# One unit's low parts by products, 2-unit turns, early loads of block 0, and array halves exchanged for odd head pairs

## The chip, the cores and the metric

The kernel runs on one core of a Trainium2 chip. The metric is the time of one execution on the device in microseconds (us). Engines are named as the profile names them: PE (TensorE, matmuls), PEld (its weight loads), DVE (VectorE), ACT (ScalarE), POOL (GpSimd) and SP (the queue that issues the DMAs).

## What is computed

A decayed linear attention and two feed-forward layers, one behind the other, in float32:

```python
def _attn_ref(q, k, v, alpha):                    # (4, 8, 768, 48) each
    for t in range(S):
        state = alpha[:, :, t, :, None] * state + einsum('bhd,bhe->bhde', k[:, :, t], v[:, :, t])
        y[:, :, t] = einsum('bhd,bhde->bhe', q[:, :, t], state)
x = y.transpose(0, 2, 1, 3).reshape(3072, 384)
x = (x @ w_a) * (x @ w_b) @ w_out                  # d_ff 1536
h = x @ w_in                                       # d_ff 2048
out = (maximum(h, 0) + alpha2 * minimum(h, 0)) @ w_out2
```

The weights come as float64.

## The kernel before

**Tiling.** The 3072 tokens are six blocks (`NB`) of 512. A block is four chunks (`BC`) of 128 time steps, one for each batch, and a chunk holds all 8 heads as 4 pairs (`NJ`). The index `g` counts the 24 chunks. In a chunk a head of a pair lies on partitions 0 to 47, the other on 64 to 111.

**Precision of the matmuls.** The feed-forward layers work on values that are split in a high and a low float32r part; `mm3` adds high*high, low*high and high*low, so a matmul of 128x128 by 128x512 is three instructions. The attention's products are plain float32: in the compiled program each is two passes, one right behind the other, so 8 products show as 16 records.

**First layer.** The weights of `w_a`, `w_b` and `w_out` are cut in 6 units (`NU1`), each of two column groups of 128. A step `k` is one column group for one block: `pa` and `pb` (9 matmuls each, `up`), their product, and 9 matmuls into three accumulators (`down1`), two steps later (`LAG`). `SEGMENTS` says in which turns the steps go: block 0 with units 0 to 2 (6 steps), block 1 with the same, both with units 3 to 5, then blocks 2 to 5 with all 6 units each. At the end of a turn `evict1` copies or adds the three accumulators to a partial sum (`part`), or splits them for the second layer.

**Weights of the first layer.** `conv` turns a float64 unit of a weight into the high and the low part: ACT takes a magnitude (L253), DVE makes four passes (`sign`, `main`, `power`, `rest`, L256 to L270), ACT rounds to the high part (L276). The low part comes in one of two ways. With `on_pe` false, DVE makes two more passes (`sub` L279, `low` L282). With `on_pe` true, PE makes a sum in PSUM (`add`, L307 to L309: identity times c1, minus identity times the high part, identity times c2) and ACT copies it (L312), in two halves for each weight. `on_pe` holds for the units 0, 1 and 2 (`PE_UNITS = 3`), each with its three weights a, b and o. Weights a and b of unit 0 are converted in two column halves; their raw words lie in the slots of weights that are needed last.

**Attention of a chunk.** DVE makes two scans and a product (`scan_r` L387, `recip`, `scan_a` L397, `mul` L402); PE transposes k (`pe_k` L440, evicted by ACT), makes A = k q (`pe_a` L457, two banks) which DVE masks (`ev_a` L464, twice), makes the change of the state (`pe_d` L481), and y (`pe_y`): `intra` (L491) is v times As with a contraction over 128, `inter` (L497) is the state Z times q with a contraction over 48. Head `i` of a pair reads partitions from 64*i and writes partitions from 64*i of one bank. ACT and DVE split y into the block's x (L564, L568). Block 0 has no `inter`; its fourth pair comes through `vg` (L508). Block 1 is `moved`: its fourth pair goes first and is brought to its place by a product with `shift` (L533). In blocks 1 to 5 kps, A0, A1, dS and y take turns on three banks (`ps_att`); in block 0 kps, A0 and A1 lie in the accumulators' banks.

**Order.** An own planner (`Graph.run`) orders all operations of all engines when the program is built: each has an estimated duration, its dependencies and a key; of those that are ready, the one with the lowest key goes first. The keys follow from `SEGMENTS`: step `k` has `at[k]`, a weight is due at the first step that uses it, and a chunk's key is `block_at[n] - (BC - c) * 7500 - 6000`. `fill` puts dummy matmuls (`wp`, L184) where the plan has PE idle. On the chip each engine goes through its list in that order.

Of the kernel before, what the change touches and what calls it, by code (L numbers as in the profile page):

```python
# [21 lines left out]
P = 128  # L22
# [5 lines left out]
    (0, 0, 3), (1, 0, 3), (0, 3, 6), (1, 3, 6),  # L28
# [4 lines left out]
PE_UNITS = 3  # L33
# [105 lines left out]
def body(tc, akq, v, vg, w_a, w_b, w_o1, w_in, w_o2, beta, out):  # L139
# [13 lines left out]
    with ExitStack() as ctx:  # L153
# [6 lines left out]
        ps_att = pool("ps_att", 3, space=PSUM)  # L160
# [62 lines left out]
        def conv(src, tag, name, key, wait, sink, early=15000, on_pe=False, halves=None):  # L223
# [14 lines left out]
            for n in range(2 if halves else 1):  # L238
# [61 lines left out]
                for h in range(2 // N):  # L300
                    cut = lambda x, h=h: x[:, :, h * UC // 2 : (h + 1) * UC // 2] if N == 1 else x
                    p = {}

                    def add(p=p, cut=cut, c1=c1, c2=c2, hi=hi):
                        t = ps_mm.tile([P, MB], F32, name="cl", tag="mm")
                        o = p["t"] = t[:, 0 : UC // 2].rearrange("p (t f) -> p t f", t=nt)
                        nc.tensor.matmul(o, ident, cut(c1()), start=True, stop=False)  # L307
                        nc.tensor.matmul(o, minus, cut(hi()), start=False, stop=False)
                        nc.tensor.matmul(o, ident, cut(c2()), start=False, stop=True)  # L309

                    def low_pe(p=p, cut=cut, lo=lo):
                        nc.scalar.copy(cut(lo()), p["t"])  # L312
                        sink(b["r"])

                    y = G.add("PE", 900, add, key, [x], pool=mpool)
# [9 lines left out]
        done, slot_of, taken = {}, {}, {}  # L325
        for u in range(NU1):
            for nm, src in (("a", w_a), ("b", w_b), ("o", w_o1)):
                x = nm, u
                slot_of[x] = len(slot_of)
                uses[x] = []  # L330

                def sink(r, x=x):
                    units[x] = as_unit(r, 2 if x[0] == "o" else KT)


                spare = {("a", 0): 3 * NU1 - 1, ("b", 0): 3 * NU1 - 2}.get(x)
                ld, done[x] = conv(src[u], f"w{slot_of[x]}", f"{nm}{u}", due[x] - 20000,
                                   taken.pop(slot_of[x], ()), sink, on_pe=u < PE_UNITS,
                                   halves=None if spare is None else (f"w{spare}", KT))
                if spare is not None:  # L340
                    taken[spare] = done[x]
# [5 lines left out]
        aring, kring, sring, yring = Ring(3), Ring(1), Ring(1), Ring(1)  # L347
# [4 lines left out]
        def chunk(g):  # L352
# [9 lines left out]

            def load_a():
                s["ra"] = tp.tile([P, 2 * NA - 1], F32, name="ra", tag="ra")
                nc.sync.dma_start(s["ra"][:, NA - 1 :], akq[g, :, 0:NA])

            def load_kq():
                s["kq"] = tp.tile([P, 2, NJ, CH], F32, name="kq", tag="kq")
                nc.sync.dma_start(s["kq"].rearrange("p s j t -> p (s j t)"), akq[g, :, NA:])
# [11 lines left out]
            la = A("SP", 800, load_a, rring.take(), 14000, 2500)  # L381
            lq = A("SP", 1500, load_kq, lring.take(), 13800, 2500, [la])
# [26 lines left out]
            rring.use(k1)  # L409
# [3 lines left out]
            if not start:  # L413
                def decayed():
                    z = Z[:, c, :, :]
                    nc.vector.tensor_tensor(out=z, in0=z, in1=r0().to_broadcast([P, NJ, D]),
                                            op=ALU.mult)

                zs = A("DVE", 360, decayed, [r, *state[c]])
                rring.use(zs)  # L420

            def ps_tile(nm, bank=None):
                if start and bank is not None:
                    return ps_acc.tile([P, NJ, CH], F32, name=nm, tag=f"acc{bank}")
                return ps_att.tile([P, NJ, CH], F32, name=nm, tag="att")

            def bank(i):

                if start:
                    w, accfree[i] = accfree[i], []  # L430
                    return w, accfree[i]
                w = aring.take()
                return w, aring.last()

            ks = None
            if not end:
                def pe_k():
                    s["kps"] = ps_tile("kps", 0)
# [7 lines left out]
                w, hold = bank(0)  # L446
# [3 lines left out]
                lring.use(x)  # L450

            def pe_a():
                s["A"] = [ps_tile(f"A{i}", i + 1) for i in range(2)]
                for j in range(NJ):
                    for i in range(2):
                        ps = slice(64 * i, 64 * i + D)
                        nc.tensor.matmul(s["A"][i][:, j, :], kT()[ps, j, :], qT()[ps, j, :],  # L457
                                         start=True, stop=True)

            def ev_a(i):  # L460
                def f():
                    s["As", i] = tp.tile([P, NJ, CH], F32, name=f"As{i}", tag=f"As{i}", bufs=1)
                    m = mask.rearrange("p (o t) -> p o t", o=1).to_broadcast([P, NJ, CH])
                    nc.vector.tensor_tensor(out=s["As", i], in0=s["A"][i], in1=m, op=ALU.mult)  # L464
                return f

            (w0, h0), (w1, h1) = bank(1), bank(2)
            pa = A("PE", 1300, pe_a, [k1, q1, *w0, *w1])
            w = sring.take()
            a0 = A("DVE", 660, ev_a(0), [pa, *w], 0, slack)  # L470
            a1 = A("DVE", 660, ev_a(1), [pa, *w], 0, slack)
            h0.append(a0)
            h1.append(a1)

            if ks is not None:
                def pe_d():
                    s["dS"] = ps_att.tile([P, NJ, D], F32, name="dS", tag="att")
# [6 lines left out]
                ds = A("PE", 500, pe_d, [ks, lv, *aring.take()])  # L484
                dhold = aring.last()
                kring.use(ds)
# [12 lines left out]

            def pe_y():  # L500
                s["y"] = ps_tile("y")
                if start:

                    for j in range(KT):
                        intra(j, j == 0, False)
                    for j in range(KT):
                        for i in range(2):
                            nc.tensor.matmul(s["y"][64 * i : 64 * i + 64, j, :], s["vg"][:, j, i, :],  # L508
                                             s["As", i][:, KT, :], start=False, stop=j == KT - 1)
# [5 lines left out]
                for j in range(NJ):  # L515
                    intra(j, j == 0, False)
                for j in range(NJ):
                    inter(j, j == NJ - 1)

            py = A("PE", 1350 if start else 500 if moved else 1600, pe_y, [a0, a1, lv, q1, zs, *aring.take()])  # L520
            yhold = aring.last()
            if moved:
                def ev_3():
                    s["y3"] = shift[:, KT, :]
                    nc.scalar.copy(s["y3"], s["y"][:, KT, :])

                def pe_m():
                    for j in range(KT):
                        intra(j, j == 0, False)
                    for j in range(KT):  # L530
                        inter(j, False)
                    for j in range(KT):
                        nc.tensor.matmul(s["y"][:, j, :], shift[:, j, :], s["y3"], start=False,  # L533
                                         stop=j == KT - 1)

                x = A("ACT", 280, ev_3, [py, *yring.take()])
                py = A("PE", 1900, pe_m, [x])
                yring.use(py)
            lring.use(pa, py)
# [20 lines left out]

            def split_h():
                if c == 0:
                    xt[n] = xpool.tile([P, 2, NJ, MB], F32R, name="x", tag="x")
                nc.scalar.copy(xt[n][:, 0, 0:nt, cols], s["y"][:, 0:nt, :])  # L564

            def split_l():
                h, l = (xt[n][:, i, 0:nt, cols] for i in range(2))
                nc.vector.tensor_tensor(out=l, in0=s["y"][:, 0:nt, :], in1=h.bitcast(F32),  # L568
                                        op=ALU.subtract)
# [146 lines left out]
        for k, (n, i, s) in enumerate(flat):  # L716
# [4 lines left out]
                            [d for j in range(k - 1) for d in done["o", flat[j][1] // 2]  # L721
                             if flat[j][1] // 2 < PE_UNITS and k < 12] + [up_before])
# [135 lines left out]
def layout(q, k, v, alpha, moe_w_a, moe_w_b, moe_w_out, moe2_w_in, moe2_w_out, moe2_alpha):  # L858
# [6 lines left out]
    def padded(x, fill):  # L865
# [12 lines left out]
    vg = np.zeros((B, CH, H * D // P, 2, 64), v.dtype)  # L878
    vg[..., D:] = (
        v[:, H - 2 :, :CH].reshape(B, 2, CH, H * D // P, 64 - D).transpose(0, 2, 3, 1, 4)  # L880
    )

    KT, GR = H * D // P, 64 - D
    rows = np.concatenate([
        np.concatenate([np.arange(D) + (2 * t + i) * D, np.arange(GR) + (2 * KT + i) * D + GR * t])
        for t in range(KT) for i in range(2)
# [27 lines left out]
```

## Time and profile before

| | us |
|---|---|
| median of 3 runs (1000.56 to 1001.47) | 1001.33 |
| the profiled execution, whole | 1001.07 |
| its span in the profile | 999.4 |
| PE busy in the span | 985.8 |
| DVE busy | 594.8 |
| ACT busy | 256.8 |
| first matmul of the first layer (block 0) | 38.18 |
| first matmul of the first layer for block 1 | 120.64 |

Times in the profile count from the start of the span. A matmul's record is longer than the time it takes from the next one, since matmuls are pipelined; the distance between starts is the cost. TensorE's granted clock is shown as a share of full speed for each stretch.

### The profile page before, as it was taken

Reading aid. Unit: us, or ns where it says so; the run is one execution under the profiler, and the core shown is the slowest. Engines: PE = TensorE matmul, PEld = TensorE weight load, DVE = VectorE, ACT = ScalarE, POOL = GpSimd, SP = SyncE. Lnnn points to the kernel's source line nnn. Section 1 sums busy time; section 2 is a strip of 40 time slices with the busy share of each in tenths; the row PEclk is TensorE's granted clock in tenths of the full one; section 3 lists DMA queues with packets and bytes.
Section 4 is the critical chain, followed back from the end, with each engine's and each line's share of the span. In section 5 each row is a group of like instructions: output and inputs, shape, how many; then the busy total and the mean of one; then the engine's idle time right before and its main releaser. Section 6 shows DMA issues by size and latency. Waiting matters only on the chain.

```text
span 999.4 us, 12894 instructions
## 1 busy us (share of the span) xinstructions
PE 985.8 (99%) x5364; PEld 794.2 (79%) x5364; DVE 594.8 (60%) x860; ACT 256.8 (26%) x421; POOL 5.5 (1%) x18
## 2 busy tenths in 40 slices
PE   6999999999999999999999999999999999999998
PEld 5776788877888888788778888888888888888886
DVE  7877798258768876884432225554554555545543
ACT  2444443232333333332122112111121111111111
POOL 2000000000000000000000000000000000000000
PEclk9999999999999999999999999999999999999999
DMA  9941200044544744551226561020020100200000
GB/s 364 362 181 53 65 12 11 1 169 117 185 155 152 252 185 147 209 195 55 64 79 221 190 221 64 1 95 1 1 95 1 64 31 1 95 1 1 32 0 32
DMA packets 30922, 103.92 MB, mean 104 GB/s; under 512 B 3472, under 2 KB 3984, under 8 KB 30864
## 3 DMA queue, kind: packets, MB, share of 16 engines
q1 hardware_dynamic: 30864, 103.11, 29.3%
q8 instruction: 42, 0.69, 0.3%
q14 instruction: 16, 0.13, 0.0%
HBM read 74.78 MB, written 26.74 MB: 102 GB/s over the span
## 4 chain that ended last, share of the span: by engine, by line
PE 99%; DVE 0%; DMA 0%; ACT 0%; issue 0%; DVEq 0%; ACTq 0%
PE acc L601 12%; PE acc L604 12%; PE acc L602 12%; PE pi L601 7%; PE pi L602 7%; PE pi L604 7%; PE pb L601 5%; PE pa L601 5%; PE pa L602 5%; PE pa L604 5%; PE pb L602 5%; PE pb L604 5%; PE A L457 3%; PE y L491 2%; PE y L497 2%; PE cl L307 1%
## 5 line engine op out<-in xcount | busy, mean ns | idle before, releaser
L624 ACT CAST gh<-ng 128x512 fp32r<-128x512 f32 x96 | 59.6, 621 | 327.6 <-DVE ng L828 275.0
L824 DVE TENSOR_SCALAR ng<-pi,betaT 128x512 f32<-128x512 f32 x96 | 72.1, 751 | 106.7 <-PE pi L604 105.8
L732 DVE TENSOR_TENSOR a_sb<-a_sb,pb 128x512 f32<-128x512 f32 x72 | 49.5, 687 | 113.8 <-PE pb L604 111.7
L628 DVE TENSOR_TENSOR gl<-ng,gh 128x512 fp32r<-128x512 f32 x96 | 66.4, 691 | 79.8 <-ACT gh L624 79.8
L601 PE MATMUL pi<-x,v 128*128 128x512 f32 x288 | 113.3, 393 | 0.0
L602 PE MATMUL acc<-gh,v 128*128 128x512 f32 x288 | 112.9, 392 | 0.0
L604 PE MATMUL acc<-gl,v 128*128 128x512 f32 x288 | 112.8, 392 | 0.0
L602 PE MATMUL pi<-x,v 128*128 128x512 f32 x288 | 112.7, 391 | 0.0
L601 PE MATMUL acc<-gh,v 128*128 128x512 f32 x288 | 112.4, 390 | 0.0
L601 PE MATMUL pb<-x,wb 128*128 128x512 f32 x216 | 87.0, 403 | 0.0
L601 PE MATMUL pa<-x,wa 128*128 128x512 f32 x216 | 86.3, 399 | 0.0
L601 PE MATMUL acc<-gh,wo 128*128 128x512 f32 x216 | 85.8, 397 | 0.0
L604 PE MATMUL acc<-gl,wo 128*128 128x512 f32 x216 | 84.9, 393 | 0.0
L602 PE MATMUL acc<-gh,wo 128*128 128x512 f32 x216 | 84.7, 392 | 0.0
L602 PE MATMUL pa<-x,wa 128*128 128x512 f32 x216 | 84.6, 392 | 0.0
L602 PE MATMUL pb<-x,wb 128*128 128x512 f32 x216 | 84.6, 391 | 0.0
L604 PE MATMUL pi<-x,v 128*128 128x512 f32 x288 | 81.5, 391 | 0.0
L729 ACT COPY a_sb<-pa 128x512 f32<-128x512 f32 x72 | 42.3, 587 | 151.3 <-PE pa L604 151.3
L624 ACT CAST gh<-a_sb 128x512 fp32r<-128x512 f32 x72 | 44.7, 621 | 132.8 <-DVE a_sb L732 132.8
L828 DVE SCALAR_TENSOR_TENSOR ng<-pi,ng 128x512 f32<-128x512 f32 x96 | 66.4, 691 | 3.1
L601 PEld LDWEIGHTS pi<-x,v 128*128 128x128 f32 x288 | 54.1, 188 | 13.8 <-DVE ng L828 2.1
L601 PEld LDWEIGHTS acc<-gh,v 128*128 128x128 f32 x288 | 54.1, 188 | 12.1
(107 smaller groups left out, 1472.4 us busy)
## 6 DMA issues: line engine op xcount, KB each, us to landing
kq<-in_akq SPq DMA_DIRECT2D x24, 512.0 KB, 3.7
w2d<-ws SPq DMA_DIRECT2D x16, 768.0 KB, 3.4
v<-w2d SPq DMA_DIRECT2D x16, 768.0 KB, 5.5
x2d<-x SPq DMA_DIRECT2D x18, 512.0 KB, 3.4
x<-x2d SPq DMA_DIRECT2D x6, 1536.0 KB, 7.0
ra<-in_akq SPq DMA_DIRECT2D x24, 258.5 KB, 2.8
v<-in_v SPq DMA_DIRECT2D x24, 256.0 KB, 4.3
rs<-in_w_in SPq DMA_DIRECT2D x8, 768.0 KB, 4.6
```

Source lines behind the costliest of these rows:

```text
L457: nc.tensor.matmul(s["A"][i][:, j, :], kT()[ps, j, :], qT()[ps, j, :], start=True, stop=True)
L491: nc.tensor.matmul(s["y"][64 * i : 64 * i + 64, j, :], s["v"][:, 2 * j + i, :], s["As", i][:, j, :], start=first, stop=last)
L497: nc.tensor.matmul(s["y"][ps, j, :], Z[ps, c, j, :], qT()[ps, j, :], start=False, stop=last)
L601: nc.tensor.matmul(o, lh, rh, start=first and n == 0, stop=False)
L602: nc.tensor.matmul(o, ll, rh, start=False, stop=False)
L604: nc.tensor.matmul(o, lh, rl, start=False, stop=last and n == len(pairs) - 1)
L624: nc.scalar.copy(gq[idx][0], src())
L628: nc.vector.tensor_tensor(out=gl, in0=src(), in1=gh.bitcast(F32), op=ALU.subtract)
L729: nc.scalar.copy(b["a"], ba["t"])
L732: nc.vector.tensor_tensor(out=b["a"], in0=b["a"], in1=bb["t"], op=ALU.mult)
L824: nc.vector.tensor_scalar(out=b["n"], in0=bh["t"], scalar1=0.0, scalar2=betaT[:, i : i + 1], op0=ALU.min, op1=ALU.mult)
L828: nc.vector.scalar_tensor_tensor(out=b["n"], in0=bh["t"], scalar=0.0, in1=b["n"], op0=ALU.max, op1=ALU.add)
```

## The change

- `on_pe` now holds for unit 0 alone (its three weights). The low parts of units 1 and 2 are made by DVE.
- The turns of blocks 0 and 1 are 2 units long: block 0 with units 0 and 1, block 1 with the same, then units 2 and 3, then 4 and 5. The rule that held a step's `up` behind the low parts of earlier units is gone.
- Chunks 2 and 3 of block 0 load alpha, k and q into four weight slots that are not in use yet, in place of the two-buffer rings; the weights of these slots load after them.
- In blocks 1 to 5 the two A tiles are one tile of two banks (`pair`), masked by one DVE instruction; y takes turns with it on the same two banks. kps and dS take turns on the one bank that is left.
- y of even pairs lies in one bank of the two and of odd pairs in the other. For odd pairs the two heads write the other half of the partitions: head `i` writes from 64 * (i ^ (j & 1)). The rows of `w_a` and `w_b` and the layout of `vg` are permuted on the host to match.
- The split of y (ACT and DVE) reads both banks; for blocks 0 and 1, which keep three pairs, it is two instructions on each engine in place of one.
- Some estimated durations for the planner change (`pe_a` 1300 to 1200, `pe_y` of block 0 1350 to 1600, `add` 900 to 1600, and others).

The core of the diff:

```diff
 SEGMENTS = (
-    (0, 0, 3), (1, 0, 3), (0, 3, 6), (1, 3, 6),
+    (0, 0, 2), (1, 0, 2), (0, 2, 4), (1, 2, 4), (0, 4, 6), (1, 4, 6),
     (2, 0, 6), (3, 0, 6), (4, 0, 6), (5, 0, 6),
 )
-PE_UNITS = 3
+ON_PE = (("a", 0), ("b", 0), ("o", 0))
...
-        ps_att = pool("ps_att", 3, space=PSUM)
+        ps_att = pool("ps_att", space=PSUM)
...
-                                   taken.pop(slot_of[x], ()), sink, on_pe=u < PE_UNITS,
+                                   taken.pop(slot_of[x], ()), sink, on_pe=x in ON_PE,
...
-        aring, kring, sring, yring = Ring(3), Ring(1), Ring(1), Ring(1)
+        aring, pring, kring, sring, yring = Ring(1), Ring(1), Ring(1), Ring(1), Ring(1)
...
+            spare = 3 * NU1 - 4 - 2 * (c - 2) if start and c >= 2 else None
+            if spare is None:
+                rwait, lwait = rring.take(), lring.take()
+                rhold, lhold = rring.last(), lring.last()
+            else:
+                rwait, lwait, rhold, lhold = (), (), [], []
+            def in_tile(nm, shape, k):
+                if spare is None:
+                    return tp.tile(shape, F32, name=nm, tag=nm)
+                return wpool.tile(shape, F32, name=nm, tag=f"w{spare + k}")
...
+            def two_banks(nm):
+                return ps_att.tile([P, 2, NJ, CH], F32, name=nm, tag="pair")
...
+                pa = A("PE", 1200, pe_a, [k1, q1, *pring.take()])
+                a0 = a1 = A("DVE", 1200, ev_a([0, 1]), [pa, *w], 0, slack)
+                pring.use(a0)
...
+            def y_of(j, rows=slice(0, P)):
+                return s["y"][rows, j % 2, j // 2, :]
             def intra(j, first, last):
                 for i in range(2):
-                    nc.tensor.matmul(s["y"][64 * i : 64 * i + 64, j, :], s["v"][:, 2 * j + i, :],
-                                     s["As", i][:, j, :], start=first, stop=last)
+                    o = 64 * (i ^ (j & 1))
+                    nc.tensor.matmul(y_of(j, slice(o, o + 64)), s["v"][:, 2 * j + i, :],
+                                     s["As"][:, i, j, :], start=first, stop=last)
             def inter(j, last):
                 for i in range(2):
-                    ps = slice(64 * i, 64 * i + D)
-                    nc.tensor.matmul(s["y"][ps, j, :], Z[ps, c, j, :], qT()[ps, j, :],
+                    ps, o = slice(64 * i, 64 * i + D), 64 * (i ^ (j & 1))
+                    nc.tensor.matmul(y_of(j, slice(o, o + D)), Z[ps, c, j, :], qT()[ps, j, :],
                                      start=False, stop=last)
...
-                            [d for j in range(k - 1) for d in done["o", flat[j][1] // 2]
-                             if flat[j][1] // 2 < PE_UNITS and k < 12] + [up_before])
+                            [up_before])
```

## Rows read from the trace of the kernel before

**Rows 1.** The page: busy time, share and instructions; shares of the last chain.
```profile
PE 985.8 (99%) x5364; PEld 794.2 (79%) x5364; DVE 594.8 (60%) x860; ACT 256.8 (26%) x421; POOL 5.5 (1%) x18
...
PE 99%; DVE 0%; DMA 0%; ACT 0%; issue 0%; DVEq 0%; ACTq 0%
```

**Rows 2.** Who waited for whom: total us, times, longest; PE's only row first.
```profile
PE kps L440 <- DVE invs L393: 8.7, 1, 8.7
...
DVE ra L387 <- DMA ra<-in_akq: 5.0, 3, 3.6
```

**Rows 3.** Busy time by stretch: length, each engine's busy us (count), PEclk, DMA, GB/s.
```profile
0.00:38.18 38.18, 29.50 (x313) 23.63 (x314) 29.46 (x47) 12.95 (x27) 5.47 (x18) 1.00 0.96 371
38.18:58.00 19.82, 19.82 (x108) 14.77 (x106) 18.14 (x28) 8.71 (x14) 0.00 (x0) 1.00 0.97 368
119.50:150.00 30.50, 30.50 (x135) 25.04 (x134) 27.63 (x39) 14.58 (x22) 0.00 (x0) 1.00 0.10 33
150.00:200.00 50.00, 50.00 (x228) 40.99 (x227) 29.18 (x42) 14.77 (x25) 0.00 (x0) 1.00 0.02 6
```

**Rows 4.** The same for DVE alone: length, busy us (count), clock, DMA, GB/s.
```profile
38.18:119.50 81.32, 62.44 (x94) 1.00 0.38 132
```

**Rows 5.** PE's timeline, 38 to 121 us: start, us, line, operation, records.
```profile
38.18 0.48 PE L601 MATMUL pa<-x,wa 128*128 128x512 f32 x1
...
42.41 0.81 PE L307 MATMUL cl<-c,plus 128*128 128x384 f32 x2
...
53.35 0.39 PE L601 MATMUL acc<-gh,wo 128*128 128x512 f32 x1
...
55.41 0.81 PE L307 MATMUL cl<-c,plus 128*128 128x384 f32 x2
...
56.88 0.49 PE L307 MATMUL cl<-c,plus 128*128 128x384 f32 x1
...
120.64 0.39 PE L601 MATMUL pa<-x,wa 128*128 128x512 f32 x1
```

**Rows 6.** Low parts on PE: all records of L307; those before 38.18 us.
```profile
L307 PE MATMUL cl<-c,plus 128*128 128x384 f32 x36 | 15.2, 505 | 0.0
...
0.00:38.18 38.18, 2.63 (x6) 0.97 (x6) 1.00 0.96 371
```

**Rows 7.** PE's timeline around one full chunk's y (chunk 8).
```profile
205.48 1.09 PE L491 MATMUL y<-As,v 128*64 128x128 f32 x16
206.50 1.08 PE L497 MATMUL y<-kq,Z 48*48 48x128 f32 x16
207.51 0.51 PE L601 MATMUL pa<-x,wa 128*128 128x512 f32 x1
```

**Rows 8.** Records of L497 in flight on PE, in slices of 0.11 us.
```profile
206.49:206.60 0.11, 0.10 (x2) 1.00 0.00 0
206.60:206.71 0.11, 0.11 (x4) 1.00 0.00 0
206.71:206.82 0.11, 0.11 (x6) 1.00 0.00 0
```

**Rows 9.** DVE's groups by line and shape: busy us, mean ns | idle before.
```profile
L464 DVE TENSOR_TENSOR As<-A,mask 128x512 f32<-128x512 f32 x48 | 31.7, 684 | 14.4 <-PE A L457 14.4
L261 DVE SCALAR_TENSOR_TENSOR c<-c,c 128x768 uint32<-128x768 uint32 x32 | 30.5, 952 | 1.5 <-ACT c L253 1.2
L402 DVE TENSOR_TENSOR kq<-kq,ra 128x1024 f32<-128x1024 f32 x24 | 29.2, 1217 | 0.0
L265 DVE TENSOR_SCALAR c<-c 128x768 uint32<-128x768 uint32 x32 | 17.7, 553 | 0.1
L279 DVE TENSOR_TENSOR c<-c,ws 128x768 f32<-128x768 f32 x16 | 15.2, 949 | 2.2 <-ACT ws L276 2.2
```

**Rows 10.** One chunk of block 1: its A on PE, its split's end on DVE.
```profile
67.26 1.16 PE L457 MATMUL A<-kq 48*128 48x128 f32 x16
...
85.22 0.56 DVE L568 TENSOR_TENSOR x<-y,x 128x384 fp32r<-128x384 f32 x1 [1.01 <-ACT x L564]
```

More of the change, by code (lines that the diff above doesn't have):

```diff
@@ L313, in low_pe @@
                         sink(b["r"])
-                    y = G.add("PE", 900, add, key, [x], pool=mpool)
+                    y = G.add("PE", 1600, add, key, [x], pool=mpool)
                     cring.use(y)
@@ L323, in as_unit @@
             return tuple(y.rearrange("p (t f) -> p t f", t=n) for y in (r[:, 0:UC], r[:, UC : 2 * UC]))
-        done, slot_of, taken = {}, {}, {}
+        done, slot_of, taken, loads = {}, {}, {}, {}
         for u in range(NU1):
@@ L337, in body @@
                 ld, done[x] = conv(src[u], f"w{slot_of[x]}", f"{nm}{u}", due[x] - 20000,
-                                   taken.pop(slot_of[x], ()), sink, on_pe=u < PE_UNITS,
+                                   taken.pop(slot_of[x], ()), sink, on_pe=x in ON_PE,
                                    halves=None if spare is None else (f"w{spare}", KT))
+                loads[slot_of[x]] = ld
                 if spare is not None:
@@ L380, in chunk @@
             r0 = lambda: s["ra"][:, 0 : NA - 1].rearrange("p (j t) -> p j t", j=NJ)[:, :, 0:1]
-            la = A("SP", 800, load_a, rring.take(), 14000, 2500)
-            lq = A("SP", 1500, load_kq, lring.take(), 13800, 2500, [la])
+            la = A("SP", 800, load_a, rwait, 14000, 2500)
+            lq = A("SP", 1500, load_kq, lwait, 13800, 2500, [la])
             lv = A("SP", 1000, load_v, vring.take(), 12000, 2500)
@@ L408, in chunk @@
             k1 = q1 = A("DVE", 1220, mul, [lq, sa], 0, slack)
-            rring.use(k1)
+            rhold.append(k1)
             zs = None
@@ L419, in chunk @@
                 zs = A("DVE", 360, decayed, [r, *state[c]])
[L420 to L425, printed above, removed]
+                rhold.append(zs)
             def bank(i):
@@ L430, in bank @@
                     w, accfree[i] = accfree[i], []
-                    return w, accfree[i]
+                    return (lambda nm: ps_acc.tile([P, NJ, CH], F32, name=nm, tag=f"acc{i}")), w, accfree[i]
                 w = aring.take()
-                return w, aring.last()
+                return (lambda nm: ps_att.tile([P, NJ, CH], F32, name=nm, tag="att")), w, aring.last()
+            def two_banks(nm):
+                return ps_att.tile([P, 2, NJ, CH], F32, name=nm, tag="pair")
             ks = None
@@ L437, in pe_k @@
                 def pe_k():
-                    s["kps"] = ps_tile("kps", 0)
+                    s["kps"] = kbank("kps")
                     for j in range(NJ):
@@ L444, in ev_k @@
                     nc.scalar.copy(s["ks"], s["kps"])
-                w, hold = bank(0)
+                kbank, w, hold = bank(0)
                 x = A("PE", 480, pe_k, [k1, *w])
@@ L449, in chunk @@
                 hold.append(ks)
-                lring.use(x)
+                lhold.append(x)
             def pe_a():
-                s["A"] = [ps_tile(f"A{i}", i + 1) for i in range(2)]
+                s["A"] = [b(f"A{i}") for i, b in enumerate(abanks)] if start else two_banks("A")
+                A = s["A"] if start else [s["A"][:, i] for i in range(2)]
                 for j in range(NJ):
@@ L456, in pe_a, with ev_a @@
                         ps = slice(64 * i, 64 * i + D)
-                        nc.tensor.matmul(s["A"][i][:, j, :], kT()[ps, j, :], qT()[ps, j, :],
+                        nc.tensor.matmul(A[i][:, j, :], kT()[ps, j, :], qT()[ps, j, :],
                                          start=True, stop=True)
-            def ev_a(i):
+            def ev_a(h):
                 def f():
-                    s["As", i] = tp.tile([P, NJ, CH], F32, name=f"As{i}", tag=f"As{i}", bufs=1)
-                    m = mask.rearrange("p (o t) -> p o t", o=1).to_broadcast([P, NJ, CH])
-                    nc.vector.tensor_tensor(out=s["As", i], in0=s["A"][i], in1=m, op=ALU.mult)
-                return f
-            (w0, h0), (w1, h1) = bank(1), bank(2)
-            pa = A("PE", 1300, pe_a, [k1, q1, *w0, *w1])
+                    if 0 in h:
+                        s["As"] = tp.tile([P, 2, NJ, CH], F32, name="As", tag="As", bufs=1)
+                    m = mask.rearrange("p (o t) -> p o t", o=1).to_broadcast([P, len(h) * NJ, CH])
+                    flat = lambda x: x.rearrange("p i j t -> p (i j) t")
+                    nc.vector.tensor_tensor(out=flat(s["As"][:, h[0] : h[-1] + 1]),
+                                            in0=s["A"][h[0]] if start else flat(s["A"]), in1=m, op=ALU.mult)
+                return f
             w = sring.take()
[L470 to L473, printed above, removed]
+            if start:
+                (b0, w0, h0), (b1, w1, h1) = bank(1), bank(2)
+                abanks = (b0, b1)
+                pa = A("PE", 1200, pe_a, [k1, q1, *w0, *w1])
+                a0 = A("DVE", 660, ev_a([0]), [pa, *w])
+                a1 = A("DVE", 660, ev_a([1]), [pa, a0])
+                h0.append(a0)
+                h1.append(a1)
+            else:
+                pa = A("PE", 1200, pe_a, [k1, q1, *pring.take()])
+                a0 = a1 = A("DVE", 1200, ev_a([0, 1]), [pa, *w], 0, slack)
+                pring.use(a0)
             if ks is not None:
                 def pe_d():
-                    s["dS"] = ps_att.tile([P, NJ, D], F32, name="dS", tag="att")
+                    s["dS"] = dbank("dS")[:, :, 0:D]
                     for j in range(NJ):
@@ L515, in pe_y @@
                 for j in range(NJ):
-                    intra(j, j == 0, False)
+                    intra(j, j < 2, False)
                 for j in range(NJ):
-                    inter(j, j == NJ - 1)
-            py = A("PE", 1350 if start else 500 if moved else 1600, pe_y, [a0, a1, lv, q1, zs, *aring.take()])
-            yhold = aring.last()
+                    inter(j, j > 1)
+            py = A("PE", 1600 if start else 600 if moved else 1600, pe_y, [a0, a1, lv, q1, zs, *pring.take()])
+            yhold = pring.last()
             if moved:
@@ L524, in ev_3 @@
                     s["y3"] = shift[:, KT, :]
-                    nc.scalar.copy(s["y3"], s["y"][:, KT, :])
+                    nc.scalar.copy(s["y3"], y_of(KT))
                 def pe_m():
                     for j in range(KT):
-                        intra(j, j == 0, False)
+                        intra(j, j < 2, False)
                     for j in range(KT):
@@ L532, in pe_m @@
                     for j in range(KT):
-                        nc.tensor.matmul(s["y"][:, j, :], shift[:, j, :], s["y3"], start=False,
-                                         stop=j == KT - 1)
+                        nc.tensor.matmul(y_of(j), shift[:, j, :], s["y3"], start=False, stop=j > 0)
                 x = A("ACT", 280, ev_3, [py, *yring.take()])
-                py = A("PE", 1900, pe_m, [x])
+                py = A("PE", 2200, pe_m, [x])
                 yring.use(py)
-            lring.use(pa, py)
+            lhold.extend((pa, py))
+            if spare is not None:
+                for k, ops in ((spare, rhold), (spare + 1, lhold)):
+                    for o in ops:
+                        o.users.append(loads[k])
+                        loads[k].need += 1
             if not end:
@@ L559, in chunk, with two @@
             vring.use(py)
+            def two(part):
+                x = xt[n][:, part, :, cols].rearrange("p (k b) t -> p b k t", b=2)
+                y = s["y"][:, :, 0 : NJ // 2, :]
+                return [(x, y)] if nt == NJ else [(x[:, :, 0], y[:, :, 0]), (x[:, 0, 1], y[:, 0, 1])]
             def split_h():
@@ L563, in split_h @@
                     xt[n] = xpool.tile([P, 2, NJ, MB], F32R, name="x", tag="x")
-                nc.scalar.copy(xt[n][:, 0, 0:nt, cols], s["y"][:, 0:nt, :])
+                for x, y in two(0):
+                    nc.scalar.copy(x, y)
             def split_l():
-                h, l = (xt[n][:, i, 0:nt, cols] for i in range(2))
-                nc.vector.tensor_tensor(out=l, in0=s["y"][:, 0:nt, :], in1=h.bitcast(F32),
-                                        op=ALU.subtract)
+                for (h, y), (l, _) in zip(two(0), two(1)):
+                    nc.vector.tensor_tensor(out=l, in0=y, in1=h.bitcast(F32), op=ALU.subtract)
             if c == 0:
@@ L878, in layout @@
     vg = np.zeros((B, CH, H * D // P, 2, 64), v.dtype)
+    KT, GR = H * D // P, 64 - D
+    swap = lambda x, j: x[::-1] if j & 1 else x
     vg[..., D:] = (
-        v[:, H - 2 :, :CH].reshape(B, 2, CH, H * D // P, 64 - D).transpose(0, 2, 3, 1, 4)
+        swap(v[:, H - 2 :, :CH].swapaxes(0, 1), KT).reshape(2, B, CH, KT, GR).transpose(1, 2, 3, 0, 4)
     )
-    KT, GR = H * D // P, 64 - D
     rows = np.concatenate([
-        np.concatenate([np.arange(D) + (2 * t + i) * D, np.arange(GR) + (2 * KT + i) * D + GR * t])
-        for t in range(KT) for i in range(2)
+        np.concatenate([np.arange(D) + (2 * t + i) * D, np.arange(GR) + (2 * KT + k) * D + GR * t])
+        for t in range(KT) for i, k in zip(swap((0, 1), t), swap((0, 1), KT))
     ])
```

16 lines of the change are left out of this document (9 added, 7 removed).

## The prediction

> **What bounds the kernel now.** I read the page first: PE is busy for 985.8 of 999.4 us, and the chain that ended last is 99% PE [rows 1]. The list of waits says how far to trust that: PE waits for another engine once, 8.7 us at the start [rows 2]. So from there on a microsecond of PE's instructions is a microsecond of time. Next I read the table of stretches: the granted clock is 1.00 throughout, so nothing is hidden in a slower clock. In the first 38.18 us PE is busy 29.50, some of it dummy matmuls, and DVE 29.46; right behind, DVE is busy 18.14 of 19.82 us, and 27.63 of 30.50 later [rows 3]. DVE is thus near its limit in the first 150 us without holding PE up, and at 29.18 of 50 us past it. Last, PE's timeline for the prices: the first step of the first layer starts at 38.18, the first one for block 1 at 120.64 [rows 5]. The change acts on that stretch, and on the y of each chunk.
>
> **Low parts that leave PE.** One sum takes 56.88 - 55.41 = 1.47 us [rows 5]. L307 has 36 records, two for each sum: 18 sums, 3 of them ahead of 38.18 [rows 6]. Unit 0 keeps 6 (two for each of three weights), so 12 go: 12 x 1.47 = 17.6 us. All 12 lie between 38.18 and 120.64, where PE never waits, so they count in full as long as DVE keeps up. DVE gets two passes of 0.95 us for each of six weights [rows 9], 11.4 us; half of that (unit 1) is needed early, the other half only after block 1's first turn. ACT loses two copies for each weight.
>
> **When block 1 can start.** With turns of 2 units block 1 is due two steps earlier. A step is 42.41 - 38.18 = 4.23 us for `pa` and `pb` and 55.41 - 53.35 = 2.06 us for the accumulators [rows 5], together 6.29, two steps 12.6. They aren't saved, they are run later; but all of block 1's attention must be done without them. Two bounds on the new start, which I call T1:
>
> PE: the 82.46 us from 38.18 to 120.64 lose 12.6, 17.6 and 0.9 (the y of block 1, below): 51.4 us. To it comes the start of the first step. DVE is idle for 38.18 - 29.46 = 8.7 us before it [rows 3], 3.6 of which is the first load; its waits for alpha come to 5.0 us [rows 2], so the early loads remove 1.4 for certain, and 5.1 at most if the planner fills every hole. That puts the first step between 33 and 37; I take 35, so T1 is 86.4 by PE (84.4 to 88).
>
> DVE: up to 119.5 it was busy for 29.46 + 62.44 = 91.9 us [rows 3, 4]. Of these, block 1's start doesn't need: the four passes of five weights of units 2 and 3, 5 x (2 x 0.95 + 2 x 0.55) = 15.0; the beginnings of two more, 3.6; two low parts of unit 3, 3.8 [rows 9]; a scan of block 2 and four products of two steps, an estimated 4.1 at the prices of L402 and L464. That leaves 65.4. New are unit 1's low parts, 6 x 0.95 = 5.7, and a second instruction in the split of 8 chunks. Its fixed part follows from L464 and L402, 0.684 us for 512 elements and 1.217 for 1024: 0.15, so 1.2 in all. The joint mask gives back 4 x (2 x 0.684 - 1.217) = 0.6 [rows 9]. Sum 71.7 us. At the occupancy that DVE reached with work waiting, 18.14/19.82 and 27.63/30.50 or 0.91 [rows 3], it is through at 3.6 + 71.7/0.91 = 82.4; the last chunk's y, shift and split behind its mask add an estimated 5. T1 is 87 by DVE.
>
> The two are almost equal, and small waits on either side add up: I take T1 = 88, with 83 and 95 as its near bounds. Against 120.64, with the two steps set off, this is 120.64 - 12.6 - 88 = 20.0 us: 17.6 by the sums, 0.9 by y, 1.5 at the start.
>
> **What the early loads push back.** Two chunks' alpha, k and q (128 x 1541 float32 each, 1.6 MB) now go ahead of unit 0's raw words on SP's queue. At 371 GB/s [rows 3] those land 4.3 us later. DVE has the four chunks to work on meanwhile, so I cost it at nothing; without that cover the first step would be 4.3 us late. Unit 4's weights wait for the borrowed slots, which are free long before its turn.
>
> **Four quarters.** A full chunk's `inter` takes 207.51 - 206.50 = 1.01 us for 8 products in 16 passes, its `intra` 1.02 [rows 7]. The slices show how: two records in the first 0.11 us, four in the second, six in the third and then no more, so two new passes start every 0.11 us and run side by side [rows 8]. Each of them uses one half of the rows and one half of the columns, so the pair leaves half of the array free. After the change two head pairs name four different quarters, and their results go to two banks. If four passes start every 0.11 us, 8 steps become 4, 0.44 us less for each of the 16 chunks of blocks 2 to 5: 6.9 us with 0.43 for each. Block 1's three pairs go from 6 steps to 4, 0.22 for each of 4 chunks: 0.9. No row shows four at once, so the bounds are 0 and 7.8 us, and below nothing if a change of quarters stopped the array (`intra` to `inter` costs about 1.01 - 8 x 0.11 = 0.13 us now). I take 7.8: the rows show the device passing over a second pass that must wait for its own quarter to start one of the next product, and nothing in that is special to two. `intra` keeps its two column halves; only their order alternates, and within one head pair both still appear, so nothing.
>
> The Trainium skill speaks against this: its page "TensorE: Matmul & The Clock Gate", section Part 3, The mechanism, says that matmuls start and end in program order, strictly first in, first out. By that the two passes of one product, which are neighbours in the program, would block the queue, and no more than two quarters would ever overlap. Here the first slice would then hold one record, not two [rows 8], so the trace doesn't agree; the result by the rule is the first rival's.
>
> **One pair of banks for A and y.** A chunk's A now waits for the split of the chunk before. In blocks 2 to 5 PE has first-layer steps to run in between, so I cost it at nothing; if it stood still instead, one mask and one split of about 0.7 us each would show for each of 16 chunks, 22 us. In block 1 it makes the four chunks a chain, which is the third rival. The longer series of partial sums (one more turn for each of blocks 0 and 1, three additions of about 0.7 us each) falls where DVE is busy 29.18 of 50 us [rows 3]: nothing.
>
> **The sum.** 1001.07 - 20.0 - 6.9 = 974.1, so 974 us. The profiled execution is 0.3 us below the median, which changes nothing.
>
> **Rivals.**
> First, quarters don't overlap beyond two: 7.8 us stay, 982 us. For it: no row shows more than two, and the order in the program. Against it: rows 8. Chance 0.15.
>
> Second, DVE sets T1 and does so badly. Over the whole stretch from 38.18 to 119.5 it was busy only 62.44 of 81.32 us, 0.77, as it stands in line behind waits for PE and ACT [rows 4]. At 0.77 the 71.7 us end at 96.7, T1 is 101.7, and the time 988. Against it: work waited less often in that stretch than it will now. Chance 0.19.
>
> Third, the other side: block 1's chain on the one pair of banks. In the row of a chunk of block 1, from A at 67.26 to the end of its split at 85.78, it took 18.5 us [rows 10], with other work let in between. Four of these in a row from 36 on give T1 = 110 and 996 us. Each further microsecond in a chunk costs 4. From 19.8 us for each chunk on nothing is left of the gain, and from 20.5 it is slower: 1004 us at 21.8. Against it: that wait came from work with lower keys, 12 sums on PE among them, that is no longer there. Chance 0.08.
>
> **How the numbers follow.** The forecast has 0.58, with T1 from 83 to 95 and 968 to 981 us of its own. The range takes in the first rival and the second, and an early T1: 965 to 990, which leaves out the third and the edges. A measurement of this kernel can tell about 0.2% (2 us) from no change. Slower by more has 0.06 and within it 0.02, both of the third rival; faster 0.92.
>
> **What the profile will show.** L307 with 12 records in place of 36, and six more passes each of L279 and L282. The slices of L497 with 4 and 8 records in the first two if four quarters run; `inter` near 0.57 us. First step at 33 to 37 and block 1's at 83 to 95; if PE has waits there, their releaser names the rival: DVE's passes the second, mask and split of block 1 the third. Wrong would be waits of PE behind 150 us, or a y that takes longer than 1.01 us.

## The result: 987.0 us, 1.4% faster, about half of the forecast gain

| | us |
|---|---|
| before, median | 1001.4 (1000.56 to 1001.94) |
| after, median | 987.01 (986.73 to 987.32) |
| ratio | 0.9857 (0.9845 to 0.9869) |
| the profiled execution of after, and its span | 986.73, 985.0 |

The forecast was 974, with a range of 965 to 990: the sign is right, the time lies in the range, the gain is 14.4 us where 27.4 were forecast. The page of after, beside [rows 1], and who PE waited for, beside [rows 2]:

```profile
PE 970.9 (99%) x5371; PEld 781.6 (79%) x5371; DVE 606.5 (62%) x866; ACT 251.9 (26%) x417; POOL 4.5 (0%) x18
...
PE kps L452 <- DVE invs L407: 8.9, 1, 8.9
PE y L521 <- DVE As L479: 0.3, 1, 0.3
```

PE still has next to no waits. So the missing 13 us must lie in what PE is busy with, and the list of its groups shows most of the new work. The columns are busy time, mean ns, idle time before:

```profile
L184 PE MATMUL wp<-ones 128*128 128x256 bf16 x125 | 16.4, 280 | 0.0
L527 PE MATMUL y<-kq,Z 48*48 48x128 f32 x320 | 14.7, 280 | 0.0
L307 PE MATMUL cl<-c,plus 128*128 128x384 f32 x12 | 5.2, 512 | 0.0
```

L307 went from 36 records [rows 6] to 12, as it should. `inter` (L527, it was L497) is 14.7 us busy, and it was 22.4 before. But the dummy matmuls (`wp`) are 125; before they were 58. They are put in by the planner, not by the chip. Busy time of L184 alone, in after, ahead of the first step, from there to block 1's first step, and behind it (a record that crosses a boundary counts on both sides):

```profile
0.00:35.27 35.27, 6.52 (x44) 1.00 0.96 369
35.27:93.83 58.56, 6.51 (x54) 1.00 0.56 205
93.83:600.00 506.17, 3.36 (x30) 1.00 0.39 134
```

Before, all but 0.25 us of them lay ahead of the first step. A stall that is filled with dummies isn't listed as a wait; it has to be looked for as work.

PE's timeline of after, the lines that answer to [rows 5]:

```profile
35.27 0.50 PE L641 MATMUL pa<-x,wa 128*128 128x512 f32 x1
...
86.89 2.25 PE L184 MATMUL wp<-ones 128*128 128x256 bf16 x19
89.07 0.44 PE L521 MATMUL y<-As,v 128*64 128x128 f32 x4
...
93.83 0.48 PE L641 MATMUL pa<-x,wa 128*128 128x512 f32 x1
...
505.99 3.12 PE L184 MATMUL wp<-ones 128*128 128x256 bf16 x27
508.87 0.48 PE L641 MATMUL pa<-x,wa 128*128 128x512 f32 x1
```

The first step comes at 35.27 (35 forecast), block 1's at 93.83 (88 forecast): 5.8 us of the miss. From there to the end the changed kernel takes 985.0 - 93.83 = 891.2 us; before's 999.4 - 120.64 = 878.8, with the two steps of 12.6 that were put off and 6.9 less for `inter`, would be 884.5. So another 6.7 us were lost behind it. 2.9 of them are the dummies from 505.99 to 508.87, ahead of block 5.

The quarters, in the slices that answer to [rows 8], and the y of one chunk, beside [rows 7]:

```profile
501.14:501.25 0.11, 0.10 (x4) 1.00 0.93 391
501.25:501.36 0.11, 0.11 (x8) 1.00 0.66 279
501.36:501.47 0.11, 0.11 (x12) 1.00 0.80 335
...
500.13 1.09 PE L521 MATMUL y<-As,v 128*64 128x128 f32 x16
501.15 0.66 PE L527 MATMUL y<-kq,Z 48*48 48x128 f32 x16
501.74 0.50 PE L641 MATMUL acc<-gh,wo 128*128 128x512 f32 x1
```

Four passes start in each 0.11 us where it was two, and `inter` takes 501.74 - 501.15 = 0.59 us in place of 1.01.

### The profile page after: what moved, and what is told of

Read it like the earlier page. It is cut to its first block, busy times and chain, and to the rows that moved or that the text cites. A ratio compares the mean times of both kernels' runs of the same rounds, so it can differ in the third digit from the quotient of the medians.

```text
span 985.0 us, 12927 instructions
## 1 busy us (share of the span) xinstructions
PE 970.9 (99%) x5371; PEld 781.6 (79%) x5371; DVE 606.5 (62%) x866; ACT 251.9 (26%) x417; POOL 4.5 (0%) x18
## 4 chain that ended last, share of the span: by engine, by line
PE 98%; DVE 1%; DMA 0%; ACT 0%; issue 0%; DVEq 0%; ACTq 0%
PE acc L641 12%; PE acc L644 12%; PE acc L642 12%; PE pi L641 7%; PE pi L642 7%; PE pi L644 7%; PE pa L641 5%; PE pb L641 5%; PE pa L642 5%; PE pb L642 5%; PE pa L644 5%; PE pb L644 5%; PE A L470 3%; PE y L521 2%; PE wp L184 1%; PE y L527 1%
```

## The experiments

Two questions were open: what eats the 13 us, and what sets block 1's first step. All are timed beside the kernel before; the times are medians of four runs, for the two with part 2 alone of ten. The kernel before, timed anew each time, had medians from 1000.75 to 1001.40 us, so differences of half a microsecond between experiments say little. The diffs show the lines that an experiment edits; `...` marks what is left out.

### The two halves of the change, each alone

Part 1 alone is the kernel before with the low parts, the 2-unit turns and the early loads; part 2 alone is the changed kernel with these three taken back (the rule on `up` and the estimate for `add` go back with them):

```diff
 # part 2 alone, from the changed kernel
-    (0, 0, 2), (1, 0, 2), (0, 2, 4), (1, 2, 4), (0, 4, 6), (1, 4, 6),
+    (0, 0, 3), (1, 0, 3), (0, 3, 6), (1, 3, 6),
...
-ON_PE = (("a", 0), ("b", 0), ("o", 0))
+PE_UNITS = 3
...
-            spare = 3 * NU1 - 4 - 2 * (c - 2) if start and c >= 2 else None
+            spare = 3 * NU1 - 4 - 2 * (c - 2) if False else None
```

> The first half of the change alone (low parts, 2-unit turns, early loads), on the attention of before: three single banks in turn, no exchange of halves. Theory C (the one pair of banks makes the chunks a chain): block 1's first step comes at 88 us or earlier in place of 93.8, there is no dummy matmul near 506 us, and the time is about 982. Theory D (DVE sets that start, the banks have no part in it): first step at 94 to 95 us and 987 to 989 in all.

> The second half alone (quarters and the pair of banks), with turns of 3 units, units 0 to 2 on PE and the old loads. Theory C: 1001.4 - 7.6 for inter + about 3 for a hole ahead of block 5 = 997. Theory D: no hole, 994.

Part 1 alone takes 989.64 us (988.76 to 990.42), part 2 alone 1001.11 (1000.71 to 1002.25; ratio to before 1.0002, 0.9993 to 1.0012). Block 1's first step of part 1 alone, on the old banks:

```profile
96.38 0.48 PE L619 MATMUL pa<-x,wa 128*128 128x512 f32 x1
```

It isn't earlier than the changed kernel's, so theory C falls for that step. The hole ahead of block 5 is as C has it: part 1 alone has no dummies near 506 us, and part 2 alone has them. But part 2 alone, with 3-unit turns, gained nothing where C expected 4 us. In its trace dummies stand ahead of block 1 (whose first step is at 125.27 in place of 120.64) and ahead of block 5; what they stand for is settled further down:

```profile
118.61 1.49 PE L184 MATMUL wp<-ones 128*128 128x256 bf16 x12
122.17 1.36 PE L184 MATMUL wp<-ones 128*128 128x256 bf16 x11
123.81 0.93 PE L184 MATMUL wp<-ones 128*128 128x256 bf16 x7
...
521.46 3.12 PE L184 MATMUL wp<-ones 128*128 128x256 bf16 x27
```

Theory D has its number for part 1 nearly (988.76 at the least) but expected 994 for part 2. Neither theory as I put it holds.

### The quarters undone, the banks kept

```diff
-                    o = 64 * (i ^ (j & 1))
+                    o = 64 * i
...
-    swap = lambda x, j: x[::-1] if j & 1 else x
+    swap = lambda x, j: x
```

> The changed kernel with the halves of odd pairs not exchanged; both banks, the order and all else stay. If four passes at once are the whole gain of that part: inter back to 1.01 us for each full chunk, 987.0 + 7.6 = 994.6. If part of it lies beside waits for the chain of chunks: 991 to 993.

It takes 994.22 us (993.33 to 995.62), 7.2 more than the changed kernel: the quarters are worth what was forecast (7.8) within 0.6. Against part 1 alone (989.64) it is 4.6 slower, and what differs between the two is the new use of the banks with what belongs to it (one pair for A and y, one bank for kps and dS, the joint mask, the split in two pieces, the planner's estimates for them). So that half gains 7.2 by its quarters and loses 4.6 of it again. The 4.6 aren't the price of the banks alone: by the traces block 1's first step even comes earlier than in part 1 alone (94.21 against 96.38), and of what is lost behind it 2.1 us are more dummies and some 1.7 a slower pace of the same matmuls, which the next section shows.

### Without dummies behind the first step

```diff
         def fill(t0, t1):
-            t = mpool.free()
+            t = None if t0 > 36000 else mpool.free()
```

The order of all other instructions on PE, DVE, ACT and POOL is the same in the two traces.

> The changed kernel without dummy matmuls behind the first step (9 us of them in the profile, between 66 and 94 us and near 506). If they stand where PE would wait anyway: 987 within 0.5, and the same 9 us as idle PE. If they are longer than the waits that they fill: 983 to 985. If the clock falls in the holes: 988 to 990 and a granted clock of 0.5 there.

It takes 981.65 us (981.56 to 981.86): 5.4 us faster than the changed kernel, more than the 2 to 4 of the second case. Where the changed kernel had dummies there are now waits, and shorter ones. PE's list:

```profile
PE kps L452 <- DVE invs L407: 8.7, 1, 8.7
PE pa L641 <- DMA x<-x: 1.4, 3, 0.6
PE y L521 <- ACT shift L555: 0.8, 2, 0.4
PE y L521 <- DVE As L479: 0.7, 1, 0.7
PE pa L641 <- ACT x L605: 0.5, 1, 0.5
PE kps L452 <- DVE Z L582: 0.4, 1, 0.4
```

Behind the start they come to 3.8 us, where the changed kernel had 9.0 of dummies (by the distance between starts, 6.1 ahead of block 1's first step and 2.9 ahead of block 5). One place shows why, the last chunk of block 1. First the mask on DVE and the end of dummies and the y in the changed kernel, then the mask and the y here:

```profile
86.41 1.22 DVE L479 TENSOR_TENSOR As<-A,mask 128x1024 f32<-128x1024 f32 x1 [0.60 <-PE A L470]
...
89.07 0.44 PE L521 MATMUL y<-As,v 128*64 128x128 f32 x4
```

```profile
85.59 1.23 DVE L479 TENSOR_TENSOR As<-A,mask 128x1024 f32<-128x1024 f32 x1 [0.54 <-PE A L470]
...
86.87 0.44 PE L521 MATMUL y<-As,v 128*64 128x128 f32 x4 [0.72 <-DVE As L479]
...
90.86 0.50 PE L641 MATMUL pa<-x,wa 128*128 128x512 f32 x1 [0.46 <-ACT x L605]
```

The mask ends at 87.63 in the one and y starts at 89.07, behind 19 dummies that stand ahead of it in PE's queue. In the other y starts 0.05 us after the mask. The dummies were sized from the planner's estimates, the chip was ahead of them, and PE ran all 19 for 1.44 us behind the end of the mask. The granted clock is 1.00 in both traces throughout these stretches: here the dummies protected nothing. The next section has a trace in which it did fall.

Some 1.8 of the 5.4 us have another source. Busy time and records of PE from 100 to 180 us, where both kernels run nothing but the first layer's matmuls, in the changed kernel and here:

```profile
100.00:180.00 80.00, 80.00 (x344) 64.81 (x343) 69.79 (x99) 31.99 (x47) 0.00 (x0) 1.00 0.02 4
```

```profile
100.00:180.00 80.00, 80.00 (x352) 65.62 (x350) 70.35 (x101) 31.93 (x47) 0.00 (x0) 1.00 0.01 4
```

344 matmuls against 352 in the same time, at the same granted clock: 8 x 0.23 = 1.8 us. The slower pace is there in the two kernels that share the changed kernel's dummies and banks with 2-unit turns (the quarters undone, 345; the loads undone, 344), and not in part 1 alone (351). Since no_fill has the order of the changed kernel but for the dummies, that order isn't what decides it. Its cause stays open.

### Is block 1's first step set by DVE or by PE?

Both start from the kernel without dummies. In the first, two passes of DVE for the weights of unit 1 are made twice; in the second, unit 1's low parts are sums on PE again.

```diff
...
-                x = G.add("DVE", d(550), sign, key, [m])
+                x = G.add("DVE", d(550), sign2 if twice else sign, key, [m])
...
-                x = G.add("DVE", d(550), power, key, [x])
+                x = G.add("DVE", d(550), power2 if twice else power, key, [x])
```

```diff
-ON_PE = (("a", 0), ("b", 0), ("o", 0))
+ON_PE = (("a", 0), ("b", 0), ("o", 0), ("a", 1), ("b", 1), ("o", 1))
```

> no_fill, with two of DVE's passes (sign and power, 0.47 us from start to start) made twice for the three weights of unit 1: 2.8 us more of DVE ahead of block 1's first step, the order of all engines unchanged. Theory D (DVE sets that step): it moves from 90.9 to 93.7 us and the time from 981.65 to 984.4. Theory E (PE's own work sets it, and DVE only shows in 2.4 us of waits): less than 1 us more.

> no_fill, with the low parts of unit 1 back on PE as well (6 sums of 1.47 us, 8.8 in all) and off DVE (5.7 us less). Theory E: block 1's first step at 96 to 98 us and the time 986 to 989. Theory D: that step at 86 to 89 us and 977 to 981.

2.8 us more on DVE cost 1.4 (983.08; 982.76 to 986.28), and the step moved from 90.86 to 91.94. 8.8 us more on PE, with 5.7 less on DVE, cost 6.9 (988.58; 987.21 to 990.09), and the step moved to 98.58. So PE's own work sets the step, with DVE a short way behind: half of what is added to DVE already shows. Theory E holds in the second but for 0.6 us of that step, and in the first it is off by 0.4 us.

The 6.9 hold a second cost. The profile of the second is of its longest run, and in it the granted clock fell, behind three waits for the moves of x ahead of block 5. The waits, and the stretch with its clock (0.50, the lower of the two levels):

```profile
509.03 0.47 PE L641 MATMUL pa<-x,wa 128*128 128x512 f32 x1 [0.29 <-DMA x<-x]
...
510.27 0.47 PE L641 MATMUL pa<-x,wa 128*128 128x512 f32 x1 [0.53 <-DMA x<-x]
...
511.56 0.69 PE L641 MATMUL pa<-x,wa 128*128 128x512 f32 x1 [0.59 <-DMA x<-x]
...
511.65:515.06 3.41, 3.41 (x9) 2.64 (x10) 0.69 (x1) 1.17 (x2) 0.00 (x0) 0.50 0.64 242
```

3.41 us at half the clock are 1.7 us lost. Two of its four runs have a mean clock of 0.997 (989.59 and 990.09); the two at 0.999 and 1.000 (987.21 and 987.58) are 5.7 above no_fill, which is the better figure for the sums. The trace of no_fill has such waits at the same place (0.34, 0.44 and 0.63 us) and keeps 1.00 there. So dummies ahead of block 5 can be worth something in some executions, less than the 5.4 us that taking them out gave.

### The early loads undone

```diff
-            spare = 3 * NU1 - 4 - 2 * (c - 2) if start and c >= 2 else None
+            spare = 3 * NU1 - 4 - 2 * (c - 2) if False else None
```

> The changed kernel with chunks 2 and 3 of block 0 loading through the two-buffer rings again. The forecast took 1.4 to 5.1 us for the early loads: first step at 36.7 to 40 us in place of 35.27 and 988.4 to 992. If something else sets block 1's first step (93.8) it comes no later: 987.0.

986.20 us (986.12 to 986.40): 0.8 less than with the early loads, hardly more than the kernel before differs between the two timings (1001.40 and 1000.86). It is no loss, where undoing the loads should have cost 1.4 to 5.1. The step that I had priced did come later, 36.82 in place of 35.27. PE's first step and block 1's, without the early loads:

```profile
36.82 0.48 PE L641 MATMUL pa<-x,wa 128*128 128x512 f32 x1
...
93.14 0.48 PE L641 MATMUL pa<-x,wa 128*128 128x512 f32 x1
```

What is won at the first step isn't there any more at block 1's. The term was read from the right row and counted at the wrong place.

### Where the banks cost, and a faster kernel

First the two halves without dummies behind the first step (the same edit to `fill`):

> part1_only without dummy matmuls behind the first step (7.4 us of them in its profile); the order of all engines is unchanged. Theory F (dummies are longer than the waits that they fill, by 5.4 of 8.7 us as between the changed kernel and no_fill): 989.64 - 4.6 = 985.0. The pair of banks then costs waits of its own: no_fill without quarters would stand near 981.65 + 7.2 = 988.9, 3.9 us above. Theory G (the pair costs only through dummies): 988 to 989.

> part2_only without dummy matmuls behind the first step (6.6 us of them, near 118 to 124 and 520 us); order unchanged. Theory F: 1001.1 - 4.1 = 997.0, the rest of the gain of the quarters lost to real waits for the chain of chunks. If the dummies are all that ate it: 993.8 to 994.5. If they only fill waits: 1001.

Part 1 without dummies takes 984.64 us (984.18 to 985.15), as theory F has it: 5.0 us of its dummies were no cover. Its first step for block 1 is at 90.92, where no_fill has 90.86. From the first step on this is 56.3 us against 55.7, and the quarters should give 0.9 there: the pair of banks costs little ahead of that step when turns are short and dummies are gone. Part 2 without dummies takes 1000.00 (999.64 to 1001.42): only 1.1 us less, and theory F misses by 3. There real waits took the place of the dummies, these at the head of the list; the two on kps and dS, which share one bank, end at 122.02 and 123.35 us, right ahead of block 1's first step at 123.95:

```profile
PE kps L452 <- DVE Z L582: 1.6, 1, 1.6
PE pa L641 <- DMA x<-x: 1.4, 3, 0.6
PE dS L503 <- ACT ks L456: 0.7, 1, 0.7
```

So with dummies gone, part 2 adds 984.64 - 981.65 = 3.0 us to part 1, of 7.2 by quarters: some 4 us are paid behind block 1's first step. Where, the next edit shows: chunks of blocks 2 to 5 earlier in the plan, so that the chain of each block ends ahead of its first step.

```diff
-            key = block_at[n] - (BC - c) * 7500 - 6000 if n else c * 1000 - 100000
+            key = block_at[n] - (BC - c) * 7500 - (6000 if n < 2 else 12000) if n else c * 1000 - 100000
```

> no_fill, with the keys of the chunks of blocks 2 to 5 lower by 6000, so that their attention is run earlier against the first layer's steps. If PE's 1.4 us of waits for the moves of x ahead of those blocks come from the chunks' chain on one pair of banks: they go, 980 to 981. If not: 981.65, or more where the earlier chunks push other work back.

It takes 979.10 us (978.52 to 979.23), 2.5 less, more than the 1.4 us of waits for the moves of x, which are gone from PE's list. The rest shows in the order on PE. From block 1's first step to the second layer dS stands right behind A in all 12 chunks that have it, as in part 1 without dummies, where no_fill has that once; and the 48 records of kps take 5.47 us by the distance between starts, in place of 6.35. So most of what the banks cost was when the chunks were run. That the waits for the moves of x come from the banks is shown, as part 1 without dummies has none; whether the other 1.1 us would also come on the old banks isn't, since these keys weren't tried on part 1 alone. Two more:

> nf_keys with block 1's chunks earlier by the same 6000 too. If block 1's first step waits for its own chunks' chain: it moves from 90.6 to 88 to 89 us, 977 to 978. If PE's own work sets it (theory E): 979 within 0.7.

> nf_keys with the loads of block 0's chunks 2 and 3 through the rings again. By no_early (986.2 against 987.0) the early loads cost 0.8 us: 978.3. If they only pay once the dummies are gone: 980 to 981.

Block 1's chunks earlier as well changes nothing: 978.52 (977.98 to 980.74), the step at PE's own pace, as theory E has it. The kernel of 979.10 without the early loads takes 977.96 us (977.78 to 978.76), the least of all, 9 us under the changed kernel (ratio to before 0.9775, 0.9759 to 0.9791).

## Why the prediction was right or wrong

**The number.** That 987 lies in the range of 965 to 990 is luck. The forecast's own range, with T1 from 83 to 95, ended at 981; the upper end was there for two rivals, and neither came. T1 alone, at 93.83, would give 980: what is above that was lost behind block 1's first step, where the sum had only a gain. Two figures of the prediction are off without bearing on its sum: T1 of 83 gives 969, not 968, and in the third rival 21.8 us for a chunk give 1009, not 1004.

**Low parts.** Right in kind, and nearly in size. Twelve sums went, and six put back cost 5.7 us (6.9 with the fall of the clock) for 8.8 us of work, while DVE got lighter by 5.7.

**Block 1's start.** 93.83 against 88, inside the near bounds of 83 to 95. The first step was right, 35.27 for 35. What failed is the count of PE's work behind it. I had 51.4 us by subtraction from [rows 5]; it was 93.83 - 35.27 = 58.6. One sum more than I had counted fell behind the first step, four in place of three (1.5 us). The rest is dummies, 6.1 us by the distance between starts less 0.4 that came out cheaper elsewhere; my sum had no term for them: the stretch that I subtracted from held 0.25 us, so I took its successor to hold none. Yet the same sum says that PE and DVE end within 1 us of each other, and the planner puts dummies where its plan has PE idle for over 500 ns (`PAUSE`). The dummies aren't all of it: without them the stretch is still 55.7 us, with 2.4 us of real waits.

**DVE.** The occupancy was right: from the first step to block 1's DVE was busy 53.66 of 58.56 us, 0.92 where I took 0.91, so the second rival with its 0.77 didn't come. The bound of 87 lies near: half of an addition shows. The last mask of block 1, put at 82.4, ended at 86.82 even without dummies.

**Quarters.** Right, mechanism and size: 7.2 measured for 7.8, the slices as forecast, 0.59 us for 0.57. The rule of the Trainium skill that I had weighed against it ("TensorE: Matmul & The Clock Gate", Part 3, The mechanism: matmuls in strict order of the program) disagrees with these slices: with the two passes of a product next to each other in the program, four in the first 0.11 us need three to be started past a pass that waits. That the two are neighbours is read from the compiled program; no trace here shows it. The first rival fell by the slices alone.

**The banks.** Wrong. I costed one pair for A and y in blocks 2 to 5 at nothing, with the first layer's steps as cover, and named 22 us if they weren't there. Mostly they were there, and PE didn't stand still for 22 us. But with dummies gone from both, part 2 adds 3.0 us to part 1 where its quarters are worth 7.2, so some 4 us are paid. At block 5's first step there was no cover: 2.9 us of dummies, or 1.4 of waits, for the moves of x that end the chain of chunks. The rest lies mostly in the changed order of kps, A and dS on PE, which the earlier keys undo. It is near the third rival's mechanism, which I had put in block 1 alone; there it showed only with 3-unit turns.

**Early loads.** The row said 1.4 us, the first step moved by 1.6, and the end didn't move with it (0.8 the other way). A start is worth something only if what ends next starts from it.

**The account of 12.6 us** between 986.73 and 974.1: 5.8 at block 1's start; 2.9 of dummies ahead of block 5; 1.8 of the slower pace. The other 2 lie, by the distances between starts from block 1's first step to the second layer, in kps (6.35 us in place of 5.47) and in the places where the first layer's matmuls are broken off for the attention, 41 in place of 35.

## What to carry to other kernels

When PE is busy for 99% of the span, look for matmuls that compute nothing before believing that it is bound by work: filler sized from a plan runs in full even when the operands are there. Taking it out is a trade: it gave 5.4 us in all here, and in one trace the clock then fell for 3.41 us. A change that shares a buffer among steps must be costed where the next work depends on the last of these steps, and by what it does to the order of the rest, not only where other work lies beside it. And a gain at a start counts only at the point from which nothing else sets the end.

## What the hardware showed that I had not expected

Float32 products on four quarters of the array start four passes in 0.11 us, though the program names them in an order in which each quarter has two in a row; before, the same holds for two. I had forecast it, but no row of before showed four.

A run of equal 512-column matmuls, with nothing between, kept one of two paces for some 90 us at a granted clock of 1.00: 344 or 352 in 80 us. The distances between starts repeat as 233, 233, 234 ns in the one and as 226, 229, 232 in the other, from the first matmuls of block 1's first step until a kps breaks the run (at 186.31 us in the changed kernel). Which pace it takes differs between kernels that issue the same matmuls there. Three explanations can be left out: the clock by its rows; the order, which no_fill shares with the changed kernel; and the dummies alone, since part 1 alone has dummies right ahead of block 1's first step and the faster pace. What decides it is open.
